# One core, a gated mix of linear attention and a spatial gating MLP: all z2 tiles ahead of z1, block sums and two queries moved, small products from VectorE to GpSimd and ScalarE

## The chip, the core and the metric

The kernel runs on one core of a Trainium2 chip. A core has five engines with a queue each: TensorE (PE; its weight loads, PEld, overlap its matmuls), VectorE (DVE), ScalarE (ACT), GpSimd (POOL) and SyncE (SP), which here only issues transfers. The metric is the device time of one launch in microseconds.

## What is computed

Two branches share one input x of 2048 tokens by 512 features, and a gate per token mixes them. Everything is bfloat16 at the boundary.

```python
g = sigmoid((x * gate_w).sum(-1, keepdims=True))
# A: linear attention, 32 heads of 16
q, k, v = heads(x @ wqkv)
pq, pk = q @ w_phi[h], k @ w_phi[h]
phi = lambda p: concat(softmax(p), softmax(-p))
kv, z = phi(pk).T @ v, phi(pk).sum(tokens)
a = ((phi(pq) @ kv) / (phi(pq) @ z + 1e-6)) @ wo
# B: spatial gating, 688 columns a half
z = gelu(x @ w_in)
z1, z2 = z[:, :688], layernorm(z[:, 688:])
b = (z1 * (w_sp @ z2 + b_sp[:, None])) @ w_out      # w_sp is 2048 by 2048
out = g * a + (1 - g) * b
```

## The kernel before, in words

The 2048 tokens are 16 tiles of 128. TensorE and ScalarE run in the order in which the program is written; the order on VectorE and GpSimd is decided by a scheduler, which follows priorities. `tc.high_priority()` raises them. A buffer of a pool is written again only when the instructions that read it before are done.

**Opening and z stage (lines 399 to 419).** x comes in transposed (xT): tiles 0 and 1 through TensorE, tiles 2 to 7 as single transposing transfers on SP's queue (`x_dma_T`, L142), tiles 8 to 11 and 12 to 15 as two large ones (L152). The weights of the second half, w_z2, are loaded first; those of the first half, w_z1, in two transfers on SP behind the x tiles 2 and 3 (L147). SP's queue then holds b_sp (brow, L155), the q and k weights, the v weights and the first three pairs of w_sp tiles (`w_load`, L170).

`z2_tile(tt)` makes eight matmuls of 344 columns (L208) into one of three PSUM buffers `zp`, then ScalarE applies Gelu (L223). One more column of the second group is the gate's logit, which VectorE copies to `glog` (L224). VectorE takes statistics of each row (`bn_stats`, L226; `bn_aggr`, L227). `z2_norm` (L285) normalizes four tiles: two small instructions on GpSimd, then four on VectorE (L292) that write z2all. `z1_tile(tt)` makes the same matmuls with w_z1 and a Gelu (L280). The stage goes through four groups of four tiles: in each, four z2 tiles, then four z1 tiles, then the norm. In the last two groups `fold` (L318) multiplies the q and k weights with w_phi on TensorE; it borrows a `zp` buffer and two more banks, which ScalarE empties (L336, L334). `b_T` (L313) turns the bias.

`z_sum(part, i)` (L391) forms sums of blocks of z2all, one VectorE instruction of 1376 columns each, eight in all: T1 to T4, two parts each. They serve the spatial product: the pairs p of row tiles (p and p + 8) in `MIXED` get their product with w_sp from seven products of half size instead of eight; the pairs in `PLAIN` (0 and 5) are multiplied plainly (`plain`, L527). Part 0 of the sums is issued in the last z1 group, part 1 in the first four iterations of the kv stage.

**kv stage (lines 712 to 741).** Iteration tt makes the k tile tt + 1 (`k_tile`, L453), the v tile tt, adds k and v of an earlier tile to the kv sums, and works off one step of the spatial products. `expo` (L437) is common to k and q: four matmuls of 512 columns (L439), two exponentials on ScalarE (L443), the sums of both softmaxes on VectorE (zs, L447, 1024 columns; the tile has two buffers). Then follow a reciprocal (rk L456, or rq L473) and `even_out` (L460): the quotient of the two sums, `ratio`, 32 columns on VectorE (L462), scales one half of the exponentials on GpSimd (L463). `v_tile` (L479) makes four matmuls (L482) into one bank, V_BANK; GpSimd copies the reciprocals beside it (L486) and VectorE scales v into `vr` (L487), which frees the bank. `q_tile` (L470) makes a query tile and sends it through a transposing transfer on SP (eqT, L476). Before, queries stand behind iterations 6, 9, 12 and 15 (`Q_AT`).

For a mixed pair the w_sp tiles are first sized (`w_size`, ScalarE, L342), leveled by a tiny matmul (`w_level`, L350, VectorE L352 and L355), scaled (`w_scale`, ScalarE, L370), and combined (`w_sum`, L372: S3 and S4 on VectorE at L358, S2 on VectorE at L377, S1 on GpSimd at L375). The products (`product`, L557, matmuls L563) go to three banks; ScalarE and VectorE (c, L570) read them, and GpSimd multiplies with z1all (L577). `prepare` issues what is due at a step, `w_size` in front of v except where tt % 3 is 2.

**Output stage (lines 746 to 797).** For each tile: attention matmuls (`attn_tile`, L604), the quotient on VectorE (rden L613, o L614), a transposing transfer, the two output products (L628, L633) and the store (L645). `FILL` lists what goes between: "p" a product, "q" a query.

Of the kernel before, what the change touches and what calls it, by code (L numbers as in the profile page):

```python
# [8 lines left out]
ALU = mybir.AluOpType  # L9
# [5 lines left out]
P = 128  # L15
# [3 lines left out]
DH = 16  # L19
F = 1376  # L20
FH = 688
HF = FH // 2
NT = S // P
NDT = D // P
CH = 512
NCH = S // CH
NFT = (FH + P - 1) // P
FPAD = NFT * P
NG = 4
# [12 lines left out]
def kernel(  # L42
# [14 lines left out]
    nc = tc.nc  # L57
# [13 lines left out]
    w_z1 = early.tile([P, NDT, FH], BF16, name="w_z1")  # L71
# [19 lines left out]
    glog = pers.tile([P, NT], FP32, name="glog")  # L91
# [16 lines left out]
    w_in_v = B_w_in.rearrange("(dt p) f -> p dt f", p=P)  # L108
# [7 lines left out]
        out=ramp[:, 0, :], data0=ones32[:, :], data1=zeros[:, :], initial=0.0,  # L116
# [4 lines left out]
    for q in range(4):  # L121
        qs = slice(32 * q, 32 * q + 32)
        nc.vector.tensor_tensor(
            out=ident[qs, qs], in0=ramp[qs, 0, :], in1=ramp[qs, 1, :], op=ALU.is_equal)
    nc.gpsimd.memset(brow[:], 0.0)
    nc.gpsimd.memset(wphi[:], 0.0)
    def load_z2w(eng, dt):
# [11 lines left out]
        out=scrap[:, :], in_=nc.const_aps.tensor(1.0, [P, 1], BF16), func=AF.Gelu_apprx_tanh)  # L139
# [3 lines left out]

    x_dma_T(2)
    x_dma_T(3)
    for h in range(2):
        nc.sync.dma_start(  # L147
            out=w_z1[:, 2 * h:2 * h + 2, :], in_=w_in_v[:, 2 * h:2 * h + 2, 0:FH])
    for i in range(4, 8):
        x_dma_T(i)  # L150
    for q in range(2, NCH):
        nc.sync.dma_start_transpose(  # L152
            out=xT[:, :, q * CH:(q + 1) * CH], in_=x2[q * CH:(q + 1) * CH, :]
        )
    nc.sync.dma_start(out=brow[0:NT, :], in_=B_b_sp.rearrange("(t p) -> t p", p=P))  # L155
    heads = A_w_phi.rearrange("(kc u) e f -> u e kc f", u=8)
    for qk in (1, 0):
# [15 lines left out]
    for p in range(NRING):  # L173
# [4 lines left out]
        out=mask4[:], in_=mask4[:], pattern=[[-32, NG]],  # L178
# [42 lines left out]
    def z2_out(tt, zp):  # L221
        z2v = z2raw[:, tt, :].rearrange("p (j n) -> p j n", j=2)
        nc.scalar.activation(out=z2v, in_=zp[:, :, 0:HF], func=AF.Gelu_apprx_tanh)  # L223
        nc.vector.tensor_copy(out=glog[:, tt:tt + 1], in_=zp[:, 1, HF:HF + 1])  # L224
        for j in range(2):
            nc.vector.bn_stats(out=bn6[:, tt, j, :], in_=z2v[:, j, :])  # L226
        nc.vector.bn_aggr(out=mv[:, tt, :], in_=bn6[:, tt, :, :].rearrange("p j s -> p (j s)"))  # L227

    def z2_tile(tt):
        z2_out(tt, z_mm(tt, w_z2, FH + 1))  # L230
# [47 lines left out]
    def z1_tile(tt):  # L278
        zp = z_mm(tt, w_z1, FH)
        nc.scalar.activation(  # L280
            out=z1_of(tt, 0, FH).rearrange("p (j n) -> p j n", j=2), in_=zp[:, :, 0:HF],
            func=AF.Gelu_apprx_tanh,
        )

    def z2_norm(ts):  # L285
        sl = slice(ts[0], ts[-1] + 1)
        nc.gpsimd.tensor_scalar(
            out=veps[:, sl], in0=mv[:, sl, 1], scalar1=1e-5, scalar2=None, op0=ALU.add
        )
        nc.gpsimd.tensor_tensor(out=rstd[:, sl], in0=veps[:, sl], in1=mhalf[:, sl], op=ALU.pow)  # L290
        for tt in ts:
            nc.vector.tensor_scalar(  # L292
                out=z2all[:, tt, :], in0=z2raw[:, tt, :],
                scalar1=mv[:, tt, 0:1], scalar2=rstd[:, tt:tt + 1],
                op0=ALU.subtract, op1=ALU.mult,
            )
# [16 lines left out]
    def b_T():  # L313
        bt = pq_tile([P, NT])
        nc.tensor.matmul(bt[:, :], lhsT=brow[:, :], rhs=ident[:, 0:NT], start=True, stop=True)
        nc.vector.tensor_copy(out=bT[:, :], in_=bt[:, :])

    def fold(qk):  # L318
        dst = (wq_p if qk == 0 else wk_p)[:].rearrange("p dt n -> p (dt n)").rearrange(
            "p (m r f) -> p r m f", r=4, f=32)  # L320
        pair = zp_tile()
        banks = [pair[:, 0, :], pair[:, 1, :], pq_tile([P, CH])[:, :], pq_tile([P, CH])[:, :]]
        for m in range(NDT * NDT):
            dt, kc = divmod(m, NDT)
            for r in range(4):
                rows = slice(32 * r, 32 * r + 32)
                nc.tensor.matmul(
                    banks[r][:, m * 32:(m + 1) * 32],
                    lhsT=wqkT[rows, qk * 4 + kc, dt * P:(dt + 1) * P],
                    rhs=wphi[rows, kc, rows], start=True, stop=True,  # L330
                )

        def take(out, in_):
            nc.scalar.copy(out=out, in_=in_.rearrange("p (m f) -> p m f", f=32))  # L334

        nc.scalar.copy(out=dst[:, 0:2], in_=pair[:, :, :].rearrange("p r (m f) -> p r m f", f=32))  # L336
        return [lambda: take(dst[:, 3], banks[3]), lambda: take(dst[:, 2], banks[2])]
# [53 lines left out]
    def z_sum(part, i):  # L391
        c = slice(4 * part, 4 * part + 4)
        out, a, op, b = Z_SUMS[i]
        nc.vector.tensor_tensor(
            out=zsums[out][:, c, :], in0=zsums[a][:, c, :], in1=zsums[b][:, c, :], op=op)
# [2 lines left out]

    with tc.manual_schedule(engines={mybir.EngineType.PE, mybir.EngineType.Activation}):
        z2_first_two()  # L400
        z2_tile(2)
        z2_tile(3)
        for c in range(NCH):
            ts = list(range(c * 4, c * 4 + 4))
            for tt in ts:
                if c > 0:
                    z2_tile(tt)
                if c >= 2 and tt % 4 == 1:
                    later = fold(3 - c)
            for tt in ts:  # L410
                z1_tile(tt)
                if c == 3:
                    z_sum(0, tt % 4)
                if c >= 2 and tt % 2 == 0:
                    later.pop(0)()
            z2_norm(ts)
            if c == 1:
                b_T()
                turn["zp"] += 1

    psA_cm.__exit__(None, None, None)
    psF_cm.__exit__(None, None, None)
# [36 lines left out]

    def even_out(e, z, rz):  # L460
        ratio = work.tile([P, H], FP32, name="ratio")
        nc.vector.tensor_tensor(out=ratio[:], in0=z[:, :, 0], in1=rz, op=ALU.mult)  # L462
        nc.gpsimd.tensor_tensor(  # L463
            out=e[:, :, 1, :], in0=e[:, :, 1, :],
            in1=ratio[:, :, None].to_broadcast([P, H, DH]), op=ALU.mult)
# [13 lines left out]
    def v_tile(tt, rk, bank):  # L479
        v_ps = bank_tile(bank)  # L480
        for dt in range(NDT):
            nc.tensor.matmul(v_ps[:, :], lhsT=xT[:, dt, tt * P:(tt + 1) * P], rhs=wv_sb[:, dt, :],  # L482
                             start=(dt == 0), stop=(dt == NDT - 1))
        vr = kvp.tile([P, 8, AW], BF16, name="vr", bufs=4)
        r0 = rk[:, :, 0].rearrange("p (u h) -> p u h", u=8)
        nc.gpsimd.tensor_copy(out=vr[:, :, 64:AW], in_=r0)  # L486
        nc.vector.tensor_tensor(  # L487
            out=vr[:, :, 0:64].rearrange("p u (h d) -> p u h d", d=DH),
            in0=v_ps[:, :].rearrange("p (u h d) -> p u h d", u=8, d=DH),
            in1=r0[:, :, :, None].to_broadcast([P, 8, NG, DH]),  # L490
            op=ALU.mult,
        )
        return vr

    def kv_acc(tt, ek, vr):
# [204 lines left out]
    def prepare(n, *kinds):  # L700
        for f, *args in work_at.get(n, ()):
            if f in kinds:
                f(*args)
# [3 lines left out]
            if f is w_scale:  # L707
                w_level(p, bank_tile(Q_BANK if n < NT else X_TAGS[2]))

    FILL = [("p", "q")] * 9 + [("p", "p"), ("p", ""), ("p", "p")] + [("", "")] * 3  # L710
    Q_AT = (6, 9, 12, 15)
    with tc.manual_schedule(engines={mybir.EngineType.PE, mybir.EngineType.Activation}):
        ks = {0: k_tile(0, Q_BANK)}
        kvacc = psM.tile([P, 8, P], FP32, name="kvacc", tag="kvat", bufs=1)
        pend = []
        for tt in range(NT):
            if tt + 1 < NT:
                ks[tt + 1] = k_tile(tt + 1, K_BANK)
            prepare(tt, w_load, load_w_out)
            if tt % 3 != 2:  # L720
                prepare(tt, w_size)
            if tt < 4:
                z_sum(1, tt)
            ek, rk = ks.pop(tt)
            pend.append((tt, ek, v_tile(tt, rk, V_BANK if tt != 1 else X_TAGS[2])))
            level(tt)
            prepare(tt, w_sum)
            if len(pend) == 3:
                kv_acc(*pend.pop(0))
            for i, part in enumerate(steps.pop(0)):  # L730
                part[0](*part[1:])
                if i == 0:
                    prepare(tt, w_scale, *[w_size] * (tt % 3 == 2))
            if tt in Q_AT:
                q_tile(Q_AT.index(tt), bank_tile(Q_BANK))
        nc.scalar.activation(out=g_el[:, :], in_=glog[:, :], func=AF.Exp)
        nc.vector.tensor_scalar(out=g_1p[:, :], in0=g_el[:, :], scalar1=1.0, scalar2=None, op0=ALU.add)
        nc.vector.reciprocal(out=g_inv[:, :], in_=g_1p[:, :])
        for p_ in pend:
            kv_acc(*p_)  # L740
        kvz_evac()
# [86 lines left out]
```

## Time and profile before

| | us |
|---|---|
| median of 3 runs (204.03 to 204.48) | 204.14 |
| the profiled execution | 203.92 |
| its span, from first to last instruction | 202.2 |
| z stage on TensorE | until 44.3 |
| kv stage | 44.3 to about 124 |
| output stage | from about 124 |
| DMA engines: moved | 26.5 MB, mean 131 GB/s |

The granted TensorE clock is at full speed over the whole span. The profile page lists busy time by engine, the waits (who stood idle, until whose instruction ended), the chain of work that ended last, and groups of instructions by line. A timeline row gives start, duration, engine, line, operation, output and inputs, and in brackets the idle time before it and its releaser. The ends of matmuls are modelled: each row is drawn longer than the time after which the next one may start, so a small idle time can be hidden, and a few matmul records are missing. The windows view gives, for stretches A:B, the busy time of PE, PEld, DVE, ACT and POOL with the number of instructions, then the granted clock, the DMA engines' busy share and GB/s.

### The profile page before, as it was taken

What the parts mean: (1) busy time and instruction counts of PE and PEld (TensorE: products, weight loads), DVE (VectorE), ACT (ScalarE), POOL (GpSimd) and SP (SyncE); (2) the same over time, 40 slices, a digit from 0 to 9 for tenths busy, and PEclk for the clock granted to TensorE, in tenths of its full rate; (3) what the DMA queues carried; (4) which work ended last, traced back from release to release, by engine and by line L of the source; (5) the groups of instructions that cost most, each with busy time, mean ns of one, the idle gap of its engine ahead of it and who ended that gap; (6) DMA issues with size and microseconds to landing.
All of it is one profiled execution on the core that took longest, in us unless ns stands there. A gap on an engine that the chain in (4) does not pass through costs nothing.

```text
span 202.2 us, 3982 instructions
## 1 busy us (share of the span) xinstructions
PE 195.5 (97%) x1474; PEld 116.7 (58%) x1491; DVE 152.2 (75%) x308; ACT 126.4 (63%) x183; POOL 85.7 (42%) x102
## 2 busy tenths in 40 slices
PE   8999999999999999999899999989999999999994
PEld 4666666665565665565465666655555555555542
DVE  4469676969979869969969995997797676675400
ACT  3466677789759489669857377775655356343222
POOL 6020202020547529658677677363345233433400
PEclk9999999999999999999999999999999999999999
DMA  5999396998034704921941926954968988896261
GB/s 197 238 178 127 67 232 134 186 209 215 2 42 93 153 3 62 224 57 29 220 88 24 187 52 167 194 111 81 165 132 168 123 184 170 166 165 137 54 153 52
DMA packets 89210, 26.50 MB, mean 131 GB/s; under 512 B 84536, under 2 KB 89064, under 8 KB 89192
## 3 DMA queue, kind: packets, MB, share of 16 engines
q1 hardware_dynamic: 86448, 23.32, 61.6%
q10 hardware_dynamic: 2600, 2.42, 4.3%
q0 software_dynamic: 144, 0.52, 0.9%
q8 instruction: 11, 0.18, 0.4%
q14 instruction: 7, 0.06, 0.1%
HBM read 3.45 MB, written 2.10 MB: 27 GB/s over the span
## 4 chain that ended last, share of the span: by engine, by line
PE 57%; DVE 27%; ACT 7%; issue 4%; DMA 2%; POOL 1%; SPq 1%; DVEq 0%; ACTq 0%
PE zp L208 15%; PE mm L563 12%; PE mm L633 10%; DVE zs L447 8%; PE mm L628 7%; PE mm L439 6%; ACT wsp L370 4%; DVE wmix L358 4%; DVE vr L487 3%; DVE rk L456 2%; DVE ratio L462 2%; PE at L604 2%; ACT wmix L342 2%; DMA eqT<-eq 2%; PE zp L239 1%
## 5 line engine op out<-in xcount | busy, mean ns | idle before, releaser
L208 PE MATMUL zp<-w_z,xT 128*128 128x344 bf16 (+1 forms) x254 | 38.5, 311 | 0.4 <-DVE glog L224 0.4
L208 PEld LDWEIGHTS <-xT 128*128 128x128 bf16 x254 | 24.6, 98 | 12.5 <-issue 0.3
L463 POOL TENSOR_TENSOR eq<-eq,ratio 128x512 bf16<-128x512 bf16 x16 | 18.2, 1136 | 28.2 <-ACT ob L645 11.5
L563 PEld LDWEIGHTS <-wsp 128*128 128x128 f16 (+1 forms) x240 | 22.9, 98 | 12.3 <-issue 0.4
L577 POOL TENSOR_TENSOR z1all<-c,z1all 128x344 bf16<-128x344 f32 x24 | 23.0, 970 | 6.6 <-DVE c L570 4.3
L443 ACT ACTIVATE eq<-mm 128x512 bf16<-128x512 f32 x32 | 17.3, 594 | 12.6 <-PE mm L439 9.0
L563 PE MATMUL mm<-z2all,wsp 128*128 128x344 f16 x144 | 23.9, 309 | 0.0
L645 ACT ACTIVATE ob<-mm,g_inv 128x512 bf16<-128x512 f32 (+1 forms) x16 | 10.9, 681 | 20.0 <-PE mm L633 17.3
L633 PE MATMUL mm<-w_out_sb,uT 128*128 128x512 bf16 (+2 forms) x102 | 23.3, 366 | 0.0
L342 ACT ACTIVATE wmix<-wsp 128x2048 bf16<-128x2048 bf16 x12 | 23.0, 1919 | 0.0
L447 DVE TENSOR_REDUCE zs<-eq 128x64 f32<-128x1024 bf16 x16 | 19.4, 1210 | 4.6 <-ACT eq L443 4.6
L463 POOL TENSOR_TENSOR ek<-ek,ratio 128x512 bf16<-128x512 bf16 x16 | 20.1, 1259 | 1.6 <-DVE ratio L462 1.1
L531 PE MATMUL mm<-z2all,wsp 128*128 128x344 f16 x128 | 20.0, 309 | 0.0
L447 DVE TENSOR_REDUCE zs<-ek 128x64 f32<-128x1024 bf16 x16 | 19.2, 1207 | 0.2 <-ACT ek L443 0.2
L443 ACT ACTIVATE ek<-mm 128x512 bf16<-128x512 f32 x32 | 17.3, 599 | 2.2 <-PE mm L439 2.2
L375 POOL TENSOR_TENSOR wsp<-wsp 128x1024 f16<-128x1024 f16 x6 | 12.7, 2123 | 13.7 <-DVE wmix L358 13.7
L439 PEld LDWEIGHTS <-xT 128*128 128x128 bf16 x128 | 11.7, 97 | 10.1
L482 PE MATMUL mm<-wv_sb,xT 128*128 128x512 bf16 x64 | 16.4, 379 | 1.0 <-DVE vr L487 0.9
L223 ACT ACTIVATE z2raw<-zp 128x688 bf16<-128x688 f32 x16 | 11.8, 744 | 7.9 <-PE zp L208 7.8
L628 PE MATMUL mm<-wo_t,oT 128*128 128x512 bf16 (+2 forms) x65 | 16.3, 366 | 0.2
L633 PEld LDWEIGHTS <-uT 128*128 128x128 bf16 x102 | 9.8, 98 | 11.2
L439 PE MATMUL mm<-wk_p,xT 128*128 128x512 bf16 x57 | 15.9, 379 | 0.4
(100 smaller groups left out, 312.4 us busy)
## 6 DMA issues: line engine op xcount, KB each, us to landing
out_dram<-ob ACTq DMA_DIRECT2D x14, 128.0 KB, 2.0
w_z<-in_B_w_in_dram SPq DMA_DIRECT2D x2, 344.0 KB, 4.1
w_out_sb<-in_B_w_out_dram SPq DMA_DIRECT2D x1, 640.0 KB, 4.5
wv_sb<-in_A_wqkv_dram SPq DMA_DIRECT2D x1, 512.0 KB
wo_t<-in_A_wo_dram POOLq DMA_DIRECT2D x1, 512.0 KB, 5.1
w_z<-in_B_w_in_dram ACTq DMA_DIRECT2D x2, 172.0 KB, 3.3
w_z<-in_B_w_in_dram SPq DMA_DIRECT2D x2, 172.0 KB, 3.2
wsp<-in_B_w_sp_dram SPq DMA_TRANSPOSE x16, 5.3
```

Of the source, the lines that this page charges most:

```text
L208: nc.tensor.matmul(zp[:, j, 0:n], lhsT=xT[:, dt, tt * P:(tt + 1) * P], rhs=wt[:, dt, j * HF:j * HF + n], start=(dt == 0), stop=(dt == NDT ...
L342: nc.scalar.activation(out=wmix[p].bitcast(BF16).rearrange("p k s c -> p (k s c)"), in_=wraw[p][:, h * NT:(h + 1) * NT, :].rearrange("p s ...
L439: nc.tensor.matmul(ps[:, :], lhsT=xT[:, dt, tt * P:(tt + 1) * P], rhs=w[:, dt, :], start=(dt == 0), stop=(dt == NDT - 1))
L443: nc.scalar.activation(out=e[:, :, a, :], in_=ps[:, :].rearrange("p (h f) -> p h f", f=DH), func=AF.Exp, scale=1.0 - 2.0 * a)
L447: nc.vector.tensor_reduce(out=z[:].rearrange("p h a -> p (h a)"), in_=e[:].rearrange("p h a f -> p (h a) f"), axis=AX.X, op=ALU.add,)
L463: nc.gpsimd.tensor_tensor(out=e[:, :, 1, :], in0=e[:, :, 1, :], in1=ratio[:, :, None].to_broadcast([P, H, DH]), op=ALU.mult)
L482: nc.tensor.matmul(v_ps[:, :], lhsT=xT[:, dt, tt * P:(tt + 1) * P], rhs=wv_sb[:, dt, :], start=(dt == 0), stop=(dt == NDT - 1))
L531: nc.tensor.matmul(x, lhsT=wraw[t % HS][:, h * NT + st, :], rhs=z2all[:, st, j * HF:(j + 1) * HF], start=(st == 0), stop=(st == NT - 1))
L563: nc.tensor.matmul(x, lhsT=w_part(p, wa)[:, st, :], rhs=zsums[zb][:, st, :], start=(k in OPENS and st == 0), stop=(st == HS - 1), skip_gro ...
L577: nc.gpsimd.tensor_tensor(out=zu, in0=o, in1=zu, op=ALU.mult)
L628: nc.tensor.matmul(acc, lhsT=oTs[n][:, g, :], rhs=wo_t[:, g, c0:c1], start=start and g == 0, stop=stop and g == NG - 1)
L633: nc.tensor.matmul(acc, lhsT=uTs[n][:, ft, :], rhs=w_out_sb[:, ft, c0:c1], start=start and ft == 0, stop=stop and ft == NFT - 1)
```

## The change

All sixteen z2 tiles come first, with a norm after every fourth, then b_T, then all sixteen z1 tiles; the eight block sums are issued among the z1 tiles, and the two folds behind z1 tiles 6 and 11. On SP's queue the two w_z1 loads move behind all of xT. The copy of the gate's logit goes from VectorE to ScalarE, `ratio` from VectorE to GpSimd, and the `vr` product gets high priority. Six queries instead of four are made in the kv stage, the two new ones behind iterations 1 and 3; the output stage makes two fewer, so `FILL` is written anew. `w_size` is put behind a step's first part where that part is product 1 or 6, instead of where tt % 3 is 2.

```diff
-    for h in range(2):
-        nc.sync.dma_start(
-            out=w_z1[:, 2 * h:2 * h + 2, :], in_=w_in_v[:, 2 * h:2 * h + 2, 0:FH])
     for i in range(4, 8):
         x_dma_T(i)
     for q in range(2, NCH):
         nc.sync.dma_start_transpose(
             out=xT[:, :, q * CH:(q + 1) * CH], in_=x2[q * CH:(q + 1) * CH, :]
         )
+    for h in range(2):
+        nc.sync.dma_start(
+            out=w_z1[:, 2 * h:2 * h + 2, :], in_=w_in_v[:, 2 * h:2 * h + 2, 0:FH])
...
-        nc.vector.tensor_copy(out=glog[:, tt:tt + 1], in_=zp[:, 1, HF:HF + 1])
+        nc.scalar.copy(out=glog[:, tt:tt + 1], in_=zp[:, 1, HF:HF + 1])
...
         z2_first_two()
-        z2_tile(2)
-        z2_tile(3)
-        for c in range(NCH):
-            ts = list(range(c * 4, c * 4 + 4))
-            for tt in ts:
-                if c > 0:
-                    z2_tile(tt)
-                if c >= 2 and tt % 4 == 1:
-                    later = fold(3 - c)
-            for tt in ts:
-                z1_tile(tt)
-                if c == 3:
-                    z_sum(0, tt % 4)
-                if c >= 2 and tt % 2 == 0:
-                    later.pop(0)()
-            z2_norm(ts)
-            if c == 1:
-                b_T()
-                turn["zp"] += 1
+        for tt in range(2, NT):
+            z2_tile(tt)
+            if tt % 4 == 3:
+                z2_norm(list(range(tt - 3, tt + 1)))
+        b_T()
+        turn["zp"] += 1
+        for tt in range(NT):
+            z1_tile(tt)
+            if tt % 2 == 1:
+                z_sum(tt // 2 // 4, tt // 2 % 4)
+            if tt in (6, 11):
+                later = fold(1 if tt == 6 else 0)
+            if tt in (7, 8, 12, 13):
+                later.pop(0)()
...
-        nc.vector.tensor_tensor(out=ratio[:], in0=z[:, :, 0], in1=rz, op=ALU.mult)
+        nc.gpsimd.tensor_tensor(out=ratio[:], in0=z[:, :, 0], in1=rz, op=ALU.mult)
...
-        nc.vector.tensor_tensor(
-            out=vr[:, :, 0:64].rearrange("p u (h d) -> p u h d", d=DH),
+        with tc.high_priority():
+            nc.vector.tensor_tensor(
+                out=vr[:, :, 0:64].rearrange("p u (h d) -> p u h d", d=DH),
...
-    FILL = [("p", "q")] * 9 + [("p", "p"), ("p", ""), ("p", "p")] + [("", "")] * 3
-    Q_AT = (6, 9, 12, 15)
+    FILL = [("p", "q")] * 6 + [("p", "qp"), ("p", "p")] + [("p", "")] * 4 + [("", "")] * 3
+    Q_AT = (1, 3, 6, 9, 12, 15)
...
-            if tt % 3 != 2:
+            late = steps[0][0][0] is product and steps[0][0][2] in (1, 6)
+            if not late:
                 prepare(tt, w_size)
-            if tt < 4:
-                z_sum(1, tt)
...
-                    prepare(tt, w_scale, *[w_size] * (tt % 3 == 2))
+                    prepare(tt, w_scale, *[w_size] * late)
```

More of the change, by code (lines that the diff above doesn't have):

```diff
@@ L486, in v_tile @@
         nc.gpsimd.tensor_copy(out=vr[:, :, 64:AW], in_=r0)
-        nc.vector.tensor_tensor(
-            out=vr[:, :, 0:64].rearrange("p u (h d) -> p u h d", d=DH),
[L489 to L492, printed above, removed]
+        with tc.high_priority():
+            nc.vector.tensor_tensor(
+                out=vr[:, :, 0:64].rearrange("p u (h d) -> p u h d", d=DH),
+                in0=v_ps[:, :].rearrange("p (u h d) -> p u h d", u=8, d=DH),
+                in1=r0[:, :, :, None].to_broadcast([P, 8, NG, DH]),
+                op=ALU.mult,
+            )
         return vr
```

## The prediction

> **What bounds the kernel now.** I read the busy table first. TensorE is the engine to beat: 195.5 of 202.2 us. The change neither adds nor removes a matmul, so all that it can win is time in which TensorE stands still, and all that it can lose is new standing time.
>
> ```profile
> PE 195.5 (97%) x1474; PEld 116.7 (58%) x1491; DVE 152.2 (75%) x308; ACT 126.4 (63%) x183; POOL 85.7 (42%) x102
> ```
>
> Second, the waits of TensorE. They are few, and they name what is late: banks that VectorE frees.
>
> ```profile
> PE mm L482 <- DVE vr L487: 0.9, 2, 0.5
> PE zp L239 <- PEq L812: 0.8, 1, 0.8
> PE at L604 <- DVE o L614: 0.6, 1, 0.6
> PE zp L208 <- DVE glog L224: 0.4, 1, 0.4
> ```
>
> Third, the timeline around one such wait (first column start, second duration).
>
> ```profile
> 77.75 2.08 POOL L577 TENSOR_TENSOR z1all<-c,z1all 128x344 bf16<-128x344 f32 x2
> 79.06 0.82 DVE L462 TENSOR_TENSOR ratio<-zs,rk 128x32 f32<-128x32 f32 x1
> 79.80 0.56 DVE L570 SCALAR_TENSOR_TENSOR c<-mm,wdown,u 128x344 f32<-128x344 f32 x1
> 80.29 1.20 DVE L447 TENSOR_REDUCE zs<-eq 128x64 f32<-128x1024 bf16 x1
> 81.41 1.20 DVE L447 TENSOR_REDUCE zs<-ek 128x64 f32<-128x1024 bf16 x1
> 82.82 1.03 PE L439 MATMUL mm<-wk_p,xT 128*128 128x512 bf16 x3
> 83.50 0.68 DVE L487 TENSOR_TENSOR vr<-mm,rk 128x512 bf16<-128x512 f32 x1
> 84.24 1.02 PE L482 MATMUL mm<-wv_sb,xT 128*128 128x512 bf16 x4 [0.39 <-DVE vr L487]
> ```
>
> The v product at 84.24 needs the bank that vr (83.50) empties. That vr's matmuls were done at about 80.2 (79.37 plus 0.86), but two reductions of 1.2 us went first on VectorE. The ratio row (0.82 us for 32 columns; the median of its 32 instructions is 0.19) ends at 79.88, just as GpSimd's z1all pair ends (79.83). Further ratios of 0.8 us or more start at 51.59, 94.97, 110.89 and 115.69, each ending within 0.05 us of the end of a GpSimd instruction.
>
> Modelled ends hide part of a stall, so I take stalls from start to start: four matmuls of 512 columns issue in 0.86 us in the chain view. 82.82 plus 0.86 is 83.68, the next starts at 84.24: **0.56**. Likewise 0.63 at 100.16, 0.26 at 63.20, and, where a product waits for the bank that c (L570) reads after a late ratio, 0.30 at 96.34 and 0.28 at 112.25. Sum in the kv stage: 2.03 us. Outside it: 0.49 at 37.27, where the z matmuls wait for a zp buffer (row below; the last fold matmul starts at 36.73, 0.05 behind it), and 0.81 at 133.79 (an attention tile waiting for o).
>
> ```profile
> 37.27 2.94 PE L208 MATMUL zp<-w_z,xT 128*128 128x344 bf16 x19 [0.35 <-DVE glog L224]
> ```
>
> All stalls after the opening: 2.03 + 0.49 + 0.81 = **3.33 us**. That is the most the change can win.
>
> **The change, part by part.** The profiled execution took 203.92 us (span 202.2 and 1.72 around it); the median of the runs, 204.14, is 0.22 above, so I add 0.22 at the end.
>
> *glog on ScalarE.* 16 copies of 0.16 leave VectorE. On ScalarE the nearest rows are the 128x1 accumulator read (0.20) and the 128x16 exponential (0.23). A z2 tile then costs ScalarE 0.74 + 0.2 = 0.94 us against 1.17 for its eight matmuls, so TensorE covers it. The stall at 37.27 goes: its buffer waited for glog on a VectorE busy with norms, and the folds now lie among z1 tiles, which need ScalarE alone. Minus 0.49. If cover failed, the excess would be paid per tile; 0.23 us is free.
>
> *All z2 first.* ScalarE and TensorE do the same work. VectorE needs per tile about 1.1 (two statistics 0.92, aggregate 0.21, overlapping slightly), so 17.6, plus 16 norms in 6.3 and eight block sums at 0.91, 7.3: 31.2 us, from 8.3 to about 40, before the stage ends near 44. Its lag holds no PSUM buffer now.
>
> *Block sums in the z1 half.* This looks like VectorE time won for the kv stage, and is worth nothing:
>
> ```profile
> 46.72 0.87 DVE L394 TENSOR_TENSOR zmix<-z2all,zmix 128x1376 f16<-128x1376 f16 x1
> 47.78 1.22 DVE L447 TENSOR_REDUCE zs<-ek 128x64 f32<-128x1024 bf16 x1 [0.18 <-ACT ek L443]
> ```
>
> The last sum ends at 47.59, and the first reduction then still waits 0.18 for ScalarE, whose table load (1.28) starts behind the last Gelu. Before and after, VectorE starts there.
>
> *x blocks sooner, w_z1 later on SP's queue.* z2 now eats one x block per 1.17 us. Tile 4's matmuls are due at 9.87 (the Gelu of the fifth tile at 11.12, minus 1.17 and 0.08), tile 8's at 14.55, tile 12's at 19.23, z1's at 23.9. SP issues the first single block at 6.00 now, after w_z1's two issues (1.1 us); it will be 4.86. Issue to landing is 2.8 us for the last single block, which has no backlog ahead: tile 4 lands at 7.6, tile 7 at 11.4. The first 512-token block is issued at 11.15 now and completes at 17.1 because of this:
>
> ```profile
> 12.00:14.50 2.50, 2.50 (x19) 1.69 (x18) 0.97 (x4) 1.49 (x2) 1.28 (x2) 1.00 0.91 208
> 15.00:17.00 2.00, 2.00 (x16) 1.37 (x14) 1.75 (x5) 1.15 (x3) 0.00 (x0) 1.00 1.27 39
> 17.00:19.00 2.00, 2.00 (x16) 1.32 (x15) 1.93 (x9) 1.45 (x2) 0.00 (x0) 1.00 0.94 212
> ```
>
> The last column is GB/s: for two microseconds the DMA engines hold packets and move almost nothing. In the DMA records this begins right after a 16 KB instruction fetch at 14.54; the first five of the block's 16 completions come at 15.0, the rest at 17.0. Issued 1.14 us sooner, the block should be complete at about 13.9, before the halt and 0.65 before it is due. The next one has until 19.23 (18.9 today). w_z1 follows by about 21, due 23.9. Cost nothing, bounds 0 and 2.55 (landing at 17.1).
>
> *vr at high priority.* Placed ahead of the reductions, it removes the 0.56, 0.63 and 0.26.
>
> *ratio on GpSimd.* VectorE loses 32 instructions, the long ones with 0.35 of issue time before them in the chain: about 1.1 us in each group of three iterations. The c instructions come earlier and the 0.30 and 0.28 go. GpSimd gains 32 small products. No row shows one: bounds 0.21 (its 128x32 cast) and 1.06 (its 128x512 product); I take 0.25, near the cast of the same width. A group of 15.9 us holds 11.5 us of GpSimd work now (76 to 92), and would hold 12.5, or 15.7 at the upper bound. A wait is added: zs has two buffers and its reader is now GpSimd, so each zs waits for the ratio of two tiles before. Behind it in VectorE's queue stand rk, vr and c. Around 91.58 GpSimd does wsp (2.12) and z1all twice (2.08) until 95.75, then the ratio, 96.0; the zs that needs it has its exponentials at 96.65. Margin 0.65, cost nothing.
>
> The row of 0.82 against 0.19 was told above. The Trainium skill, "SBUF — State Buffer", "Who interferes with whom", says that a VectorE instruction with two SBUF inputs and a reading GpSimd instruction exclude each other for their whole length. By that rule the move only changes who waits. Against the change speaks "GPSIMD Engine Reference", "4.1 Engine selection": about twice VectorE's time for two inputs, so an estimated 0.38 us; the sum would stay.
>
> *Two queries at iterations 1 and 3.* TensorE work is moved, not added (two times 0.86). VectorE gets twice zs 1.13 and rq 0.26, 2.8 us, and loses 1.5 us of ratios there, in a window that grows by TensorE's 1.7. SP gets two eqT transposes ahead of the weight loads issued at 62.27 and 77.89; those wait for TensorE's reads anyway. The output stage loses the two and stays bound by TensorE. At 133.79 S3 (L358, 2.09 beside GpSimd) still precedes o: I leave that 0.81. The `late` rule moves one w_size behind a product, cost nothing.
>
> **Sum.** 203.92 − 2.03 − 0.49 = 201.40; plus 0.22 is 201.62, plus 0.1 for small waits that the denser TensorE meets: **201.7**.
>
> **Rivals.**
> 1. *The queries eat the relief* (chance 0.18). VectorE is busy 4.00 of 4.00 us in 48 to 52 and 52 to 56. If half of the 2.03 comes back, 202.7; still faster.
> 2. *The 0.81 goes too* (0.12): everything won, 200.9. For it: VectorE reaches S3 without a ratio before it. Against: S3 waits for ScalarE.
> 3. *x is late* (0.08). If the halt catches the first large block, tile 8 waits 2.55, which cancels the 2.52: 204.2, the same. It decides from 0.65 us of delay.
> 4. *GpSimd's queue holds VectorE* (0.12): the other side. If GpSimd runs over 0.65 us late at the ratio behind wsp and z1all, zs, and all behind it, waits. ek rows of 2.04 against 1.06 show that it can lose 0.98 at once. Then the kv stage's stalls stay and three groups lose 0.98 each: 204.14 − 0.49 + 2.94 = 206.6.
>
> My forecast has 0.50. Faster by over 0.2% (about what a measurement of this kernel can tell): 0.50 + 0.18 + 0.12 = 0.80; within 0.2%: 0.08; slower: 0.12. The range, 200.8 to 204.3, takes in all but rival 4.
>
> **What would show it.** Right: TensorE's start-to-start gaps in the kv stage under 0.1 us, no wait for vr or glog; ratio rows on GpSimd near 0.25; zs never released by GpSimd; last sum before 44. Wrong: a TensorE gap near 14.5 released by a transpose of x; zs waiting for ratio; a c or vr still late.

## The result and the profile after

| | before | after |
|---|---|---|
| median of 6 runs, us | 204.08 (203.29 to 204.48) | 202.31 (201.92 to 203.11) |
| ratio to before, 95% interval | | 0.9918 [0.9894, 0.9943] |
| the profiled execution, us | 203.92 | 202.68 |
| its span, us | 202.2 | 200.3 |
| outside the span, us | 1.72 | 2.38 |
| k tile 0 to attention tile 0 on TensorE, us | 81.78 | 81.87, with two queries more |

The changed kernel is faster by 1.77 us in the medians and by 1.9 us in the span; 201.7 had been forecast. The time outside the span was between 1.81 and 2.47 us in the six runs, so a part of their scatter lies there.

The busy row of the page, then the waits view of TensorE (time in all, times, longest). In the page's row VectorE's share falls from 75 to 70%, GpSimd's rises from 42 to 46%:

```profile
PE 194.9 (97%) x1473; PEld 116.8 (58%) x1491; DVE 139.5 (70%) x260; ACT 126.7 (63%) x199; POOL 93.0 (46%) x134
```

```profile
PE zp L239 <- PEq L807: 0.8, 1, 0.8
PE at L600 <- DVE o L610: 0.4, 1, 0.4
PE zp L208 <- DMA w_z<-in_B_w_in_dram: 0.3, 1, 0.3
```

No wait for vr or glog is left; the third row is the first weight load of the opening, which landed 0.6 us later than in the trace of before and is the same code in both. Counted from start to start as in the prediction, the stalls behind the opening fell from 3.33 to 1.13 us: 0.55 at 133.56 (an attention tile that waits for o, 0.81 before), and three new pairs of 0.19 to 0.21 at 76.65, 91.81 and 106.99, 0.58 together. 2.2 us won, less about 0.4 that the opening came later (the 126th z matmul starts at 23.41, at 23.03 before), is 1.8; the last instruction ends 1.96 earlier.

The timeline of the changed kernel at the place that the prediction read, where the v product had waited 0.56 us. The v product of the next iteration is the last row:

```profile
81.64 1.22 DVE L442 TENSOR_REDUCE zs<-eq 128x64 f32<-128x1024 bf16 x1 [0.59 <-ACT eq L438]
81.65 0.27 POOL L457 TENSOR_TENSOR ratio<-zs,rk 128x32 f32<-128x32 f32 x1
82.78 0.68 DVE L483 TENSOR_TENSOR vr<-mm,rk 128x512 bf16<-128x512 f32 x1
...
83.63 1.16 DVE L442 TENSOR_REDUCE zs<-ek 128x64 f32<-128x1024 bf16 x1
...
84.26 1.03 PE L434 MATMUL mm<-wk_p,xT 128*128 128x512 bf16 x4
...
85.13 1.03 PE L477 MATMUL mm<-wv_sb,xT 128*128 128x512 bf16 x4
```

Two things are to be seen. VectorE idles here, 0.59 us in the brackets, where it had been late. And v follows k after 0.87 us, the issue time of four matmuls: nothing stands between them. The gain, though the last instructions show it, is earned here: the stretch from the first k tile to the first attention tile is as long as before and holds two queries (2 × 0.86 us) more.

### The profile page after: what moved, and what is told of

Its sections match the earlier page's. It is cut to its first block, busy times and chain, and to the rows that moved or that the text cites. A ratio compares the mean times of both kernels' runs of the same rounds, so it can differ in the third digit from the quotient of the medians.

```text
span 200.3 us, 3991 instructions
## 1 busy us (share of the span) xinstructions
PE 194.9 (97%) x1473; PEld 116.8 (58%) x1491; DVE 139.5 (70%) x260; ACT 126.7 (63%) x199; POOL 93.0 (46%) x134
## 4 chain that ended last, share of the span: by engine, by line
PE 89%; DVE 4%; ACT 3%; DMA 2%; issue 1%; SPq 0%; DVEq 0%
PE mm L559 24%; PE zp L208 19%; PE mm L434 12%; PE mm L629 10%; PE mm L624 7%; PE mm L477 6%; PE mm L527 6%; PE at L600 2%; DMA w_z<-in_B_w_in_dram 2%; PE kvacc L494 2%; ACT wmix L342 2%; DVE zs L442 1%; DVE o L610 1%; DVE wmix L358 1%; ACT eq L438 0%
## 5 line engine op out<-in xcount | busy, mean ns | idle before, releaser
L375 POOL TENSOR_TENSOR wsp<-wsp 128x1024 f16<-128x1024 f16 x6 | 12.8, 2126 | 13.8 <-DVE wmix L358 13.8
L457 POOL TENSOR_TENSOR ratio<-zs,rk 128x32 f32<-128x32 f32 x16 | 7.5, 466 | 23.7 <-DVE rk L451 21.1
L458 POOL TENSOR_TENSOR eq<-eq,ratio 128x512 bf16<-128x512 bf16 x16 | 16.9, 1058 | 1.3
L458 POOL TENSOR_TENSOR ek<-ek,ratio 128x512 bf16<-128x512 bf16 x16 | 16.9, 1059 | 0.0
```

What stands on the lines that cost most here:

```text
L375: S1_ENG.tensor_tensor(out=a21, in0=a21, in1=a22, op=ALU.add)
L458: nc.gpsimd.tensor_tensor(out=e[:, :, 1, :], in0=e[:, :, 1, :], in1=ratio[:, :, None].to_broadcast([P, H, DH]), op=ALU.mult)
```

## The experiments

Every ratio below is to the kernel before, run on the same chip. The theory after the result was that VectorE's queue in the kv stage, not one late instruction, was the bound; the rival was the prediction's own account, in which vr's place, c's delay and glog each carry their own stall.

### vr at high priority, alone

```diff
-        nc.vector.tensor_tensor(out=vr[:, :, 0:64]...
+        with tc.high_priority():
+            nc.vector.tensor_tensor(out=vr[:, :, 0:64]...
```

> The kernel before, with the high priority on vr alone. Theory A (each edit removes its own gaps of TensorE, as priced: 0.56, 0.63 and 0.26 us are vr's): these three go, the two gaps behind c (0.30, 0.28), the 0.49 at the folds and the 0.81 at the attention tile stay: 1.45 us less, 202.6 us. Theory B (either edit on VectorE's kv chain is enough, since any slack lets all of it run earlier): nearly all of 2.03 us goes, 202.1. Theory C (vr only changes places with a reduction, and the next instruction in the queue is late instead): under 0.5 us, 203.6 or more.

204.08 us, ratio 1.0004 [0.9984, 1.0025]: nothing. The v stalls are gone and the kv stage does get shorter: first k to first attention tile takes 80.87 us, 0.9 less than before. It isn't 1.45, since 0.23 at 90.27 and 0.55 at 105.93 appear where a product waits for a bank: ScalarE's u, which empties it, stands behind a 2 us w_scale that started 0.09 us after VectorE's wup, at 87.69. The 0.9 is then lost again, as the attention tile's stall doubles. The timeline of this run:

```profile
121.77 2.42 POOL L578 TENSOR_TENSOR z1all<-c,z1all 128x344 bf16<-128x344 f32 x3
123.04 1.18 DVE L347 TENSOR_TENSOR wsum<-wsum 128x1 bf16<-128x1 f32 x1 [0.88 <-ACT wmix L342]
124.14 0.68 DVE L505 TENSOR_TENSOR kvz<-kvacc,mask 128x512 bf16<-128x512 f32 x1
...
133.60 0.41 PE L605 MATMUL at<-kvz,eqT 128*128 128x68 bf16 x8 [1.45 <-DVE o L615]
```

The stall of 0.81 became 1.62 (start to start). wsum, one column, took 1.02 us longer here than the 0.16 of the run with ratio moved, and ended as GpSimd's z1all ended; from there to o VectorE stands idle for only some 0.1 us, so the delay reaches o. What is put first makes other instructions of the queue late. The step "vr at high priority removes 0.56, 0.63 and 0.26" held as a description of those stalls and failed as a price.

### ratio on GpSimd, alone

```diff
-        nc.vector.tensor_tensor(out=ratio[:], in0=z[:, :, 0], in1=rz, op=ALU.mult)
+        nc.gpsimd.tensor_tensor(out=ratio[:], in0=z[:, :, 0], in1=rz, op=ALU.mult)
```

> The kernel before, with ratio on GpSimd alone. Theory A: the two gaps behind c go (0.58 us), vr's stay: 203.5. Theory B: VectorE has about 1.1 us more room in each group of three iterations, so vr is no longer late either: 2.03 us less, 202.1. Theory C: zs now waits for GpSimd and the gain is lost: 204.1 or more, with zs rows released by ratio.

202.04 us, 0.9908 [0.9885, 0.9931]: the whole gain, from one line, and without vr's priority. All five stalls that the prediction listed in the kv stage are gone, v's as well as c's; one of 0.2 is new, at 66.05, where a product waits for a bank that ScalarE empties. 0.51 at 36.85 (glog) stays, and o's is 0.54 at 131.20 instead of 0.81. So 2.03 less 0.2, plus 0.27, is 2.1 by the stalls. First k to first attention tile takes 79.88 us, 1.9 less than before. VectorE's rows at the place that the prediction read, then the v product on TensorE, 0.86 behind k:

```profile
78.45 0.56 DVE L570 SCALAR_TENSOR_TENSOR c<-mm,wdown,u 128x344 f32<-128x344 f32 x1
79.28 1.22 DVE L447 TENSOR_REDUCE zs<-eq 128x64 f32<-128x1024 bf16 x1 [0.27 <-POOL z1all L577]
80.42 1.21 DVE L447 TENSOR_REDUCE zs<-ek 128x64 f32<-128x1024 bf16 x1
82.23 0.68 DVE L487 TENSOR_TENSOR vr<-mm,rk 128x512 bf16<-128x512 f32 x1
```

```profile
82.21 1.03 PE L439 MATMUL mm<-wk_p,xT 128*128 128x512 bf16 x3
83.07 1.03 PE L482 MATMUL mm<-wv_sb,xT 128*128 128x512 bf16 x4
```

### The three edits of engines and priority, old order

The two edits above and `nc.scalar.copy` for glog, with the old order of tiles, block sums, loads and queries.

> The kernel before with only the three edits of engine and priority: glog on ScalarE, ratio on GpSimd, vr at high priority; the old order of z2 and z1, block sums, loads, queries and FILL. Theory A (the new order of tiles, block sums and queries is worth nothing by itself): as fast as the changed kernel, 202.3 to 201.6. Theory D (the order is needed): at least 0.5 us slower than the changed kernel, with a gap at the folds near 37 or the first kv iterations late.

201.29 us, 0.9873 [0.9849, 0.9896]. The stall at the fold is gone, as predicted for glog; 0.25 at 65.55 and 0.54 at 130.65 are what is left. So no gain of the reordering of tiles, sums, loads and queries is seen on top. Against the changed kernel the comparison was repeated side by side (below).

### The changed kernel with the old places of the queries

```diff
-    FILL = [("p", "q")] * 6 + [("p", "qp"), ("p", "p")] + [("p", "")] * 4 + [("", "")] * 3
-    Q_AT = (1, 3, 6, 9, 12, 15)
+    FILL = [("p", "q")] * 9 + [("p", "p"), ("p", ""), ("p", "p")] + [("", "")] * 3
+    Q_AT = (6, 9, 12, 15)
```

> The changed kernel with the old places of the queries (after iterations 6, 9, 12, 15, and the old FILL). Theory A: TensorE-bound in both stages, so 1.72 us of work moves to the output stage and the time is that of the changed kernel within 0.2 us. Theory D (the gain comes from the emptier output stage): slower by 0.5 us or more, with gaps in the output stage.

201.59 us, 0.9897 [0.9863, 0.9930]. In the trace the three pairs of small stalls are gone, 0.58 us of TensorE; the times alone, with overlapping intervals, don't separate the two. What the pairs were is in the changed kernel's timeline:

```profile
74.06 2.00 ACT L370 ACTIVATE wsp<-wsp,wup 128x2048 f16<-128x2048 bf16 x1 [0.99 <-DVE wup L355]
75.97 0.62 ACT L541 ACTIVATE u<-mm,bT,wdown 128x344 f32<-128x344 f32 x1
76.64 1.33 PE L559 MATMUL mm<-zmix,wsp 128*128 128x344 f16 x8
```

The product at 76.64 needs the bank that ScalarE's u reads until 76.59, and u stands behind a 2 us w_scale that waited for VectorE's wup. From the leveling matmul to w_scale it takes 3.27 us here and 2.72 with the old queries.

### The changed kernel with ratio back on VectorE

> The changed kernel with ratio back on VectorE. Theory P (the gain of the kv stage is that VectorE's small product with two SBUF inputs no longer stands behind GpSimd's long ones; vr's priority adds little): at least 1.2 us slower than the changed kernel, 203.5 to 204.2, with ratio rows of 0.8 us again. Theory A (as forecast, vr's priority keeps its 1.45 us and only the gaps behind c come back): 0.58 us slower, 202.9.

204.39 us, 0.9993 [0.9970, 1.0016]. All the rest of the change together is worth nothing without the one line. The ratio rows beside GpSimd are long again (0.65 to 0.77, four of them), and the stalls are those of vr alone: 0.50 at 91.87, 0.55 at 107.53, 1.62 at 135.22. The waits view of this run also has a row for x, in the opening that is the same code as after's:

```profile
PE at L600 <- DVE o L610: 1.5, 1, 1.5
...
PE zp L208 <- DMA xT<-in_A_x_dram: 0.5, 1, 0.5
```

That wait is not what made the run slower: from the 126th z matmul, which comes after it, to the end of VectorE's last instruction its trace takes 176.32 us, 174.42 after and 176.76 before.

### Does ratio's lock matter, or its time?

The 32 ratios took 8.94 us on VectorE before, of which some 3.2 were what five long rows took beyond 0.19. Is it these waits beside GpSimd that cost, or any 9 us? ratio goes to GpSimd, and a reciprocal that nobody reads takes its place: one SBUF input, 0.29 us, 32 times, 9.4 us.

```diff
+        spare = work.tile([P, H], FP32, name="spare")
+        nc.vector.reciprocal(out=spare[:], in_=z[:, :, 1])
```

> The kernel before with ratio on GpSimd, and in its place on VectorE a reciprocal of 32 columns whose result nobody reads: one SBUF input, 0.35 us by the row of rq, 32 times, so VectorE is given more work (11.2 us) than the 32 ratios took from it (10.2 us at most by the rows' own long waits, 6 without). Theory P (what the ratio cost was the waiting behind GpSimd, in the middle of a chain): still at least 1.2 us faster than before, 202.0 to 202.8. Theory I (what counts is the time that VectorE is busy): 204.0 or more.

205.28 us, 1.0043 [1.0017, 1.0068], against 0.9908 without the spare work: the gain is gone, and more. The waits view, then the timeline at the first of the two:

```profile
PE mm L484 <- DVE vr L489: 2.1, 2, 1.1
```

```profile
79.86 1.21 DVE L447 TENSOR_REDUCE zs<-eq 128x64 f32<-128x1024 bf16 x1
80.99 1.21 DVE L447 TENSOR_REDUCE zs<-ek 128x64 f32<-128x1024 bf16 x1
82.11 0.34 DVE L475 RECIPROCAL rq<-zs 128x32 f32<-128x32 f32 x1
82.37 0.29 DVE L467 RECIPROCAL spare<-zs 128x32 f32<-128x32 f32 x1
82.58 0.49 DVE L456 RECIPROCAL rk<-zs 128x64 f32<-128x64 f32 x1
83.00 0.29 DVE L467 RECIPROCAL spare<-zs 128x32 f32<-128x32 f32 x1
83.21 0.73 DVE L347 TENSOR_TENSOR wsum<-wsum 128x1 bf16<-128x1 f32 x1
83.86 0.68 DVE L489 TENSOR_TENSOR vr<-mm,rk 128x512 bf16<-128x512 f32 x1
```

The rows touch: no brackets, no idle time, and vr is late again without a single ratio on VectorE. But the test is not clean, since wsum's 0.73 is itself a wait beside GpSimd: it was 0.10 with ratio alone, and it ends at 83.94, with this row of GpSimd (83.93):

```profile
82.87 1.06 POOL L463 TENSOR_TENSOR eq<-eq,ratio 128x512 bf16<-128x512 bf16 x1
```

So 0.63 of the stall here (1.12 at 84.59) comes from it, and as much of the other (1.26 at 101.35). First k to first attention tile takes 83.23 us, 3.35 more than with ratio alone; less the two waits of wsum an estimated 2.1 is left, about the 1.9 that ratio's move had won. Theory P, by which the gain stays, fell: plain work of the same length in ratio's place costs about what ratio had cost, so VectorE's queue is what counts. A wait beside GpSimd is time in that queue too; how much of the ratio's own cost was its waits is not shown apart.

### The loads of w_z1 ahead of x tile 4 again

```diff
     x_dma_T(3)
+    for h in range(2):
+        nc.sync.dma_start(
+            out=w_z1[:, 2 * h:2 * h + 2, :], in_=w_in_v[:, 2 * h:2 * h + 2, 0:FH])
...
-    for h in range(2):
-        nc.sync.dma_start(
-            out=w_z1[:, 2 * h:2 * h + 2, :], in_=w_in_v[:, 2 * h:2 * h + 2, 0:FH])
```

> The changed kernel with the two w_z1 loads back between the x tiles 3 and 4. Theory X (x is then late for a z2 half that eats a block per 1.17 us): tile 4 lands at 10.35 and is due at 9.87; the large block lands at 17.1 because of the halt of the DMA engines and is due at 14.55, so TensorE stands still for about 2.6 us in all: 204.9. Rival: the loads are not what x waits for, within 0.3 us of the changed kernel.

203.35 us, 0.9953 [0.9928, 0.9977], 1.0 us above after. The waits view of this run:

```profile
PE zp L208 <- DMA xT<-in_A_x_dram: 1.6, 2, 1.2
```

The first stall is 1.33 us at 10.63 (a single x block, landed at 10.58), the second 0.56 at 15.87 (the first large one, landed at 15.82). The mechanism is right, the size was not: the 17.1 for the large block was its landing in the trace of before, where the halt of the DMA engines began behind a 16 KB instruction fetch at 14.54. Here the block landed 1.3 us sooner, and the fetch came at 17.77, behind it, though the transfers dropped to 47 GB/s in 16.0 to 16.5: that the fetch makes the halt is not shown. The 1.89 us cost 1.1 at the 126th z matmul (24.51, 23.41 after), since TensorE had come to full pace 0.8 earlier in this run (6.37, 7.18 after). From there to the end both traces take 174.42 us.

### The logit's copy back on VectorE

> The changed kernel with the glog copy back on VectorE. Theory V (all z2 first makes VectorE the slower of the two: four tiles with their norm take it about 6.3 us against 4.7 on TensorE, and the copy then holds the zp buffers): three groups lose 4.8 us, two spare buffers give back 2.3, so about 2.5 us slower than the changed kernel, 204.8. Rival (as in the kernel before, only one gap near the folds): 0.3 us slower at most, 202.6.

208.87 us, 1.0211 [1.0160, 1.0262], 6.6 above after in the medians and 5.4 in the profiled executions (208.12 and 202.68), where 2.5 had been expected. The waits view, then VectorE's rows at one of the three stalls:

```profile
PE zp L208 <- DVE glog L224: 5.8, 3, 2.6
```

```profile
27.09 1.56 DVE L292 TENSOR_SCALAR z2all<-z2raw,mv,rstd 128x688 f16<-128x688 bf16 x4 [1.09 <-POOL rstd L290]
28.57 0.20 DVE L227 BATCH_NORM_AGGREGATE mv<-bn 128x2 f32<-128x12 f32 x1
28.69 0.10 DVE L224 COPY glog<-zp 128x1 f32<-128x1 f32 x1
```

A copy of 0.10 us holds a zp buffer while VectorE waits for GpSimd's rstd and does a norm. With z2 alone in the stage TensorE asks for a norm every 4.7 us, with no z1 tile between to give VectorE time, and the norms here start 6.6 us apart (20.53, 27.09). The edit that the prediction priced at 0.49 is what the new order needs in order to cost nothing.

### Side by side: the changed kernel, the three edits, and o sooner

The last question was whether a version beats both. Four kernels ran on one chip. The third splits S3 of pair 6 on the three edits, the fourth does so on the changed kernel with the old queries:

```diff
+        elif k == 3 and p == 6:
+            for c in (slice(0, HS // 2), slice(HS // 2, HS)):
+                w_mul_sub(s3[:, c], w_part(p, "A11")[:, c], p, a21[:, c])
         elif k == 3:
             w_mul_sub(s3, w_part(p, "A11"), p, a21)
```

> The changed kernel once more, beside e10 to e12 on one chip, so that they are compared with it directly. Expected: 202.3 us, plus or minus 0.3, with the stall of 0.55 us ahead of the attention tile at 133.6 and three pairs of small stalls (0.58 us in all) where product 4 waits for ScalarE's u. If the differences of 0.7 and 1.0 us that e4 and e3 showed came from the chip or the opening and not from the kernels, this one lies near 201.5 and beside them.

> The kernel before with the three engine edits (vr at high priority, ratio on GpSimd, the logit's copy on ScalarE) and the old order, the same as e3, as the control of e11. If the order of tiles, the block sums and the two early queries are worth nothing or cost a little: 201.3 us, 0.6 to 1.0 below e9. If e3 only had a lucky opening: within 0.3 of e9.

> e10 with S3 of pair 6 in two instructions of half the columns, so that the attention quotient o need not stand behind one instruction of 2 us on VectorE. It computes the same. Theory A: the stall of 0.54 us at about 131 is o standing behind S3; with half the length it falls to 0.1 or less, and the time is 200.8 us, 0.4 below e10. Theory B: o waits for something else that is as late (S3 runs beside GpSimd and both halves still go first), the stall stays or moves to the next tile: 201.2, the same as e10. An extra fixed cost of the second instruction would show as 0.1 or less.

> The changed kernel with the old places of the queries (as e4) and S3 of pair 6 in two halves (as e11). Theory A (o behind S3 makes the stall): 201.1 us, 0.4 to 0.5 below e4's 201.6 and 1.2 below e9. Theory B (the stall moves on): 201.6, 0.7 below e9. If the new order of the tiles is worth something after all, it lies below e11; if it is worth nothing, within 0.3 of e11.

| | us | ratio |
|---|---|---|
| changed kernel | 202.08 | 0.9912 [0.9894, 0.9930] |
| three edits | 201.78 | 0.9901 [0.9884, 0.9919] |
| three edits, split | 202.84 | 0.9945 [0.9921, 0.9970] |
| changed, old queries, split | 202.73 | 0.9942 [0.9925, 0.9959] |

The three edits lie 0.3 us below the changed kernel and the intervals overlap; the 1.0 us that separated them in the earlier sets of runs did not return. From the 126th z matmul to the end, which leaves the opening out, their traces take 174.50 and 174.46 us. So no version found is shown to beat the changed kernel, and three of its edits do all that it does.

The split made things worse by 1.1 us, which neither theory had. The stall of 0.54 did go, and one of 1.80 came at the next tile, at 135.45. VectorE's rows and GpSimd's S1 in the trace of the three edits:

```profile
128.96 1.97 DVE L358 SCALAR_TENSOR_TENSOR wmix<-wsp,wup 128x1024 f16<-128x1024 bf16 x1
130.85 0.74 DVE L615 SCALAR_TENSOR_TENSOR o<-at,g_el,rden 128x512 bf16<-128x512 f32 x1
...
133.60 0.62 DVE L377 TENSOR_TENSOR wmix<-wsp,wmix 128x1024 f16<-128x1024 f16 x1
```

```profile
131.01 2.12 POOL L375 TENSOR_TENSOR wsp<-wsp 128x1024 f16<-128x1024 f16 x1 [1.16 <-DVE wmix L358]
```

and with the split, VectorE's rows, then GpSimd's:

```profile
127.95 1.44 DVE L358 SCALAR_TENSOR_TENSOR wmix<-wsp,wup 128x512 f16<-128x512 bf16 x1
129.31 0.74 DVE L618 SCALAR_TENSOR_TENSOR o<-at,g_el,rden 128x512 bf16<-128x512 f32 x1
...
131.10 0.73 DVE L358 SCALAR_TENSOR_TENSOR wmix<-wsp,wup 128x512 f16<-128x512 bf16 x1
...
132.68 1.96 DVE L377 TENSOR_TENSOR wmix<-wsp,wmix 128x1024 f16<-128x1024 f16 x1
134.56 0.74 DVE L618 SCALAR_TENSOR_TENSOR o<-at,g_el,rden 128x512 bf16<-128x512 f32 x1
```

```profile
131.97 2.12 POOL L375 TENSOR_TENSOR wsp<-wsp 128x1024 f16<-128x1024 f16 x1 [3.13 <-DVE wmix L358]
```

o got its place between the halves, 0.54 us sooner counted from the first k tile. But GpSimd's S1 (L375) waits for the second half, so it starts 1.97 us later, counted the same way, and VectorE's S2 (L377) now starts inside it: 1.96 us instead of 0.62, done 0.55 behind the end of S1 (134.09). The next tile's o stands behind it. The Trainium skill, "SBUF — State Buffer", "Who interferes with whom", has this as a rule: a VectorE instruction with two SBUF inputs and a GpSimd instruction that reads SBUF block each other, and the second one waits for the whole of the first. These rows agree with it.

## Why the prediction was right, and where it was not

Direction and size held: 2.44 us was forecast on the medians, 1.77 measured, and 202.31 lies in the range. The account of where it comes from did not hold, so that the sum came out near is in part luck: the 1.45 us put down to vr, which won nothing alone, was made up by ratio, which won 2.04 where 0.58 stood, and the queries took 0.58 that was not in the sum.

- **vr at high priority** (1.45 of the 2.52): failed as a cause. Alone it won nothing. The prediction looked at which instruction was late and not at how long the queue was; moving one forward leaves the queue as long. 0.9 us of the kv stage was won and 0.8 lost again at o, behind a wsum that waited beside GpSimd.
- **ratio on GpSimd** (0.58): the mis-sized term. Alone it won 2.04 us, vr's stalls included. Its working took out only the stalls behind a late c, while the 32 rows of 8.94 us, and the reductions that start sooner, were what vr had waited for too. The typical row was priced well: medians 0.25 and 0.27 us against an estimate of 0.25. Six rows of 0.71 to 1.25 raise the mean to 0.40, 12.9 us in all where 8.0 had been put down. The estimate by the Trainium skill, "GPSIMD Engine Reference", "4.1 Engine selection", about twice VectorE's time or 0.38, lies above the medians; against VectorE's 0.19 they are 1.3 to 1.4 times.
- **glog on ScalarE** (0.49): right, the copy took 0.15 and the stall went. Its larger role, that z2 first would cost 5 to 7 us without it, was not seen.
- **Block sums**: right. The last one ends at 40.7 instead of 47.6, and the first reduction starts at 47.73 instead of 47.78.
- **z2 first, x**: right in that it cost nothing: no x wait in the trace of after. The first large block landed at 14.33, estimated 13.9; the opening of this trace came later, and TensorE began tile 8 at 14.78 instead of 14.55. 0.45 us is a thin margin: in the trace of the kernel with ratio back the block landed at 14.55, and TensorE waited 0.65 for it. Rival 3 was nearer than its chance of 0.08 says.
- **Two queries**: priced at nothing, cost 0.58 in stalls by the traces. This is rival 1 in part, by another way: through ScalarE's u, not through vr.
- **The stall ahead of o**: left at 0.81, measured 0.55. ratio's move alone brings it to 0.54, so the shrinking belongs to that edit. That S3 is what o waits for is shown: with S3 halved o came 0.54 sooner.
- **Rival 4**, GpSimd holding VectorE: did not happen. No zs waits for a ratio. GpSimd does lose time, but TensorE does not wait for it, as two rows of the timeline after show:

```profile
85.62 1.18 DVE L358 SCALAR_TENSOR_TENSOR wsp<-wsp,wup,wmix 128x1024 f16<-128x1024 bf16 x1
85.78 1.15 POOL L457 TENSOR_TENSOR ratio<-zs,rk 128x32 f32<-128x32 f32 x1 [0.56 <-DVE rk L451]
```

Here ratio is the one that is held, ending 0.13 behind the VectorE row, as a 0.82 row had been held by GpSimd before. The prediction's reading that the move changes who waits was right; it matters because GpSimd has room in this stage and VectorE's queue had none.

Open: whether vr's priority adds anything once ratio has moved. With both and glog the kernel is at 0.9873 and 0.9901 in two sets of runs, ratio alone at 0.9908; the fold's stall of 0.5 us is 0.0025 of that, and the rest is within the intervals. The traces say the same: from the 126th z matmul to the end they take 174.18 and 174.46 us with the three edits, and 174.67 with ratio alone, the fold's 0.5 included.

## What to carry to other kernels

When several instructions of one engine are late in turn, suspect that engine's queue in that stage as the bound: here a priority only chose who waits, and taking small work off the queue cleared them all. Price such a move by the stalls of everything behind it, and test the parts alone, since here one line of many carried the gain. Before splitting or moving an instruction on VectorE, look what GpSimd will be doing at the time to which it, and what follows it, moves.

## What was not expected of the hardware

- A VectorE product of one column with two SBUF inputs (wsum), 0.16 us in the run with the three edits, took 1.18 with vr's priority alone, beside GpSimd's z1all, ending within 0.03 us of it. What the instruction holds up counts, not its size: the stall ahead of o grew by 0.8 in that run.
- The same kernel, that of the three edits, started its 126th z matmul at 22.47 us in one trace and at 23.60 in another. 0.84 of that is a wait of TensorE at 5.84, for the transfer of the gate's weights (gaterow), which the first trace does not have. Differences of a microsecond between single traces have to be taken from a mark behind the opening.
